# Attention scores on two opposite 64x64 quarters of the array, from the queries as loaded

## The chip, the cores and the metric

The kernel runs on one core of a Trainium2 chip (trn2). The metric is the device time of one execution in microseconds, the median of several runs. Its engines are named as in the profile: PE (TensorE; PEld are its weight loads), DVE (VectorE), ACT (ScalarE), POOL (GpSimd) and SP (SyncE, which here only starts transfers).

## What is computed

The reference chains an attention and two mixtures of experts. Only the attention is touched here:

```python
def _attn_ref(q, k, v):                      # 4 batches, 8 heads, 768 positions, 64 wide
    block, window = (32, 16)
    k_sum = k.reshape(B, H, nb, block, D).max(axis=3)
    v_sum = v.reshape(B, H, nb, block, D).mean(axis=3)
    scores_l = scale * q @ k^T               # only where |i - j| < window
    scores_s = scale * q @ k_sum^T + log(block)
    a = softmax(concat(scores_l, scores_s))
    return a @ concat(v, v_sum)
...
x = moe(attention)      # top-1 routing, 8 experts, tokens with a positive skip score
x = moe2(x)             # capacity-bound routing, 8 experts
```

So a query sees 31 neighbouring keys and the 24 block maxima of its head; its output is a mean over the neighbouring values and the 24 block means.

## The kernel before

`phase_a` computes the attention in eight units (a batch and one of two groups of four heads) of six steps each, 48 steps in all. Partitions 0 to 63 hold the 64 dimensions of one pair of heads, partitions 64 to 127 those of the other pair, so a tile row carries two heads at once. `load(u)` starts a unit's transfers on SP: keys `kt`, queries `qd`, values for the means `vt` (a `wraw` tile), and values for the product `VV`.

A step is a software pipeline; loop i emits on each engine, in this order, `qk(i)`, `ptr(i-2)`, `ex(i-1)`, `pv(i-3)`, then the work behind the attention:
- `qk` (lines 121 to 130): four score matmuls into `s_ps`. The 128 stationary columns are 64 queries of head A and 64 of head B; the moving operand has 118 columns, 24 block maxima and 94 neighbouring keys. VectorE adds the mask and takes the maximum (line 129).
- `ex` (131): ScalarE's exponentials. `ptr` (137): four transposes into `pt_ps`, ScalarE copies them to `pt_sb`. `pv` (144): eight product matmuls into `o_ps`, 64 columns wide, on the two column halves in turn; VectorE divides by the row sum into `X`.
- `post` (162) and `logits` (168): for odd units, whose tile then holds all 512 columns, transposes of a finished row block, four 32-column matmuls with the routing weights, and one more transpose. The bank `l_ps` exists once.

Since one stationary operand holds both heads, it has to be block diagonal: `Q2` holds zeros in two quarters (memset, line 69), and `prep_q` (106) copies the loaded queries into the other two, one half by ScalarE and one by VectorE. Keys are needed at offsets 64 columns apart, each with the 24 maxima in front, so `prep_k` (95, VectorE) takes the maxima, `prep_k2` (98) copies the neighbouring keys of odd windows into `K2`, and `prep_kc` (102, lines 104 and 105) copies the maxima in front of the windows in `kt` and `K2`. For units 2 to 7 all of these are VectorE's except one half of `prep_q`; the tables `SHIFT1` and `SHIFT` say in which step of the unit before they are emitted.

The block means: `add_v` (109) halves `vt` five times (VectorE for units 0 and 1, POOL after), `mean_v` (114) turns the sums with two transposes into an `l_ps` bank (line 117), ScalarE scales them (118), and three POOL copies spread them into `VV` (119). `AT_S` and `AT_M` say in which loop; both are emitted ahead of `pv`. In loop 5, `spin` keeps PE at work with four matmuls on the identity (line 243).

```python
229    AT_S={2:0,6:1,**{NT*u-5:u for u in range(2,8)}}; AT_M={3:0,7:1,**{NT*u-2:u for u in range(2,8)}}
...
244        if i in AT_S: add_v(AT_S[i])
245        if i in AT_M: mean_v(AT_M[i])
246        for j in pvs.get(i,[i-LB] if q+3<=i<n+LB else []): pv(j)
247        logits(i-PL-1)
```

After step 47 the routing, the gathered first expert layer (`phase_b`) and the second one (`phase_d`) follow; they start from the attention's last rows.

Of the kernel before, what the change touches and what calls it, by code (L numbers as in the profile page):

```python
# [11 lines left out]
NT=6  # L12
# [5 lines left out]
WARM=11; KEEP=(5,4)  # L18
SHIFT1=(2,3,3,3,4); SHIFT=(0,2,2,1,4)
# [30 lines left out]
def phase_a(nc,tc,ctx,I,st):  # L50
# [8 lines left out]
    Q2=[]; VV=[]; K2=[cp.tile([128,2,NT,118],F32,name=f"K2_{i}") for i in range(2)]  # L59
# [6 lines left out]
    for i in range(2):  # L66
        t=cp.tile([128,2,12,128],F32,name=f"Q2_{i}"); Q2.append(t)
        for h in range(2):
            (G if i else V).memset(t[0:64,h,:,64:128],0.0); G.memset(t[64:128,h,:,0:64],0.0)
# [8 lines left out]
    def load(u):  # L78
        b,g=units[u]
        kt=ld.tile([128,2,KW],F32,name="kt",bufs=3); qd=ld.tile([128,2,S],F32,name="qd"); vt=st["raw"].tile([128,2048],F32,name="wraw")  # L80
        vv=VV[u%3]; src=I['v65']
        def ld_k(h0,h1): nc.sync.dma_start(kt[:,h0:h1],I['k'][b,:,2*g+h0:2*g+h1,:])
        def ld_q(h0,h1): nc.sync.dma_start(qd[:,h0:h1],I['q'][b,:,2*g+h0:2*g+h1,:])
        def ld_v():
            nc.sync.dma_start(vt[:,0:1536],I['vt'][b,:,g])
        def ld_vv():
            for s0 in (0,2): nc.sync.dma_start(vv[24:24+VP,3*s0:3*s0+6].rearrange("p (a s) h d -> p a (s h d)",s=3),src[b,g,:,s0:s0+2,0:780])
        U[u]=dict(kt=kt,qd=qd,vt=vt,vv=vv,q2=Q2[u%2],k2=K2[u%2])
        U[u]['ks']=wk.tile([128,2,24],F32,name="ks",bufs=2)
# [16 lines left out]
    def prep_q(u,h,half,cpy):  # L106
        d=U[u]; qd,q2=d['qd'],d['q2']; r=64*half
        cpy(q2[r:r+64,h,:,r:r+64],qd[r:r+64,h].rearrange("p (t c)->p t c",c=64))  # L108
# [5 lines left out]
    def mean_v(u):  # L114
        d=U[u]; vt=d['vt']; ms=vt[0:24,1536:1792]
        p=ps.tile([128,4,128],F32,name="l_ps",bufs=1)
        for h in range(2): T.transpose(p[0:24,h,:],vt[:,1800+24*h:1824+24*h],ident)
        A.mul(ms.rearrange("p (h d)->p h d",d=128),p[0:24,0:2,:],1.0/32)  # L118
        for w in (0,4,8): G.tensor_copy(d['vv'][0:24,w:w+4,:,0:64],ms.rearrange("p (h d)->p h d",d=64)[:,None].to_broadcast([24,4,4,64]))  # L119
    X={}; XT={}; D={}  # L120
    def qk(i):
        u,pairs=steps[i]; d=U[u]
        p=ps.tile([128,4,128],F32,name="s_ps")
        for j,(h,w) in enumerate(pairs):
            T.matmul(p[:,j,0:118],d['q2'][:,h,w,:],d['k2'][:,h,w//2,:] if w%2 else d['kt'][:,h,64*w:64*w+118],start=True,stop=True)  # L125
# [42 lines left out]
    def logits(i):  # L168
# [3 lines left out]
        if not (now or old): return  # L172
# [49 lines left out]
    def first(u,h):  # L222
        prep_k(u,h); prep_k2(u,h,A.copy); prep_kc(u,h,V.tensor_copy)
        prep_q(u,h,0,A.copy); prep_q(u,h,1,V.tensor_copy)
# [4 lines left out]
    AT_S={2:0,6:1,**{NT*u-5:u for u in range(2,8)}}; AT_M={3:0,7:1,**{NT*u-2:u for u in range(2,8)}}  # L229
    splits={-1:((0,1),),0:((0,2),(0,3)),1:((1,0),(1,1)),2:((1,2),(1,3))}  # L230
    for i in range(n+PL+3):
# [11 lines left out]
        if i==KEEP[0]: spin(KEEP[1],ident.bitcast(BF)[:,None,:].to_broadcast([128,2,256]))  # L243
        if i in AT_S: add_v(AT_S[i])
        if i in AT_M: mean_v(AT_M[i])
        for j in pvs.get(i,[i-LB] if q+3<=i<n+LB else []): pv(j)
# [7 lines left out]
        if i<n and u and u+1<8:  # L254
# [881 lines left out]
```

## Time and profile before

| | |
|---|---|
| median of 3 runs | 668.12 us (667.36 to 669.19) |
| the profiled execution | 666.73 us |
| its span | 664.8 us |
| mean granted TensorE clock | 0.949 |
| PE busy | 597.6 us (90%) |
| VectorE busy | 457.9 us (69%) |
| ScalarE busy | 326.7 us (49%) |
| POOL busy | 363.3 us (55%) |
| weight loads (PEld) busy | 489.3 us (74%) |

The execution's own time is 1.9 us above its span, the first to the last instruction. Busy shares are averages over stages: the attention takes about the first quarter of the span, and there the waits between engines have to be read step by step. A matmul's end is modelled, and matmuls overlap, so the distance between starts tells what one costs, not its duration.

### The profile page before, as it was taken

Reading aid. Unit: us, or ns where it says so; the run is one execution under the profiler, and the core shown is the slowest. Engines: PE = TensorE matmul, PEld = TensorE weight load, DVE = VectorE, ACT = ScalarE, POOL = GpSimd, SP = SyncE. Lnnn points to the kernel's source line nnn. Section 1 sums busy time; section 2 is a strip of 40 time slices with the busy share of each in tenths; the row PEclk is TensorE's granted clock in tenths of the full one; section 3 lists DMA queues with packets and bytes.
Section 4 is the critical chain, followed back from the end, with each engine's and each line's share of the span. In section 5 each row is a group of like instructions: output and inputs, shape, how many; then the busy total and the mean of one; then the engine's idle time right before and its main releaser. Section 6 shows DMA issues by size and latency. Waiting matters only on the chain.

```text
span 664.8 us, 12679 instructions
## 1 busy us (share of the span) xinstructions
PE 597.6 (90%) x4465; PEld 489.3 (74%) x4468; DVE 457.9 (69%) x1689; ACT 326.7 (49%) x712; POOL 363.3 (55%) x395
## 2 busy tenths in 40 slices
PE   7859898998889999998349979999999999999994
PEld 4747776877567777775328869788887978898983
DVE  7957898889887799693876736677776767652110
ACT  5646685786644856661035144261625445363510
POOL 3163455162146388972038086393948759397941
PEclk9877898999989999999579999999999999999998
DMA  8997577505616978710071450907245170845000
GB/s 283 338 301 221 186 281 206 179 2 216 247 33 218 363 261 267 235 67 25 1 229 74 158 191 1 326 23 267 83 164 182 62 275 17 300 172 193 33 17 32
DMA packets 47616, 111.83 MB, mean 168 GB/s; under 512 B 3937, under 2 KB 4705, under 8 KB 47552
## 3 DMA queue, kind: packets, MB, share of 16 engines
q1 hardware_dynamic: 38992, 85.87, 38.4%
q0 software_dynamic: 6208, 20.39, 9.0%
q10 hardware_dynamic: 2352, 4.76, 2.0%
q8 instruction: 36, 0.59, 0.4%
q14 instruction: 28, 0.23, 0.1%
HBM read 96.53 MB, written 14.88 MB: 168 GB/s over the span
## 4 chain that ended last, share of the span: by engine, by line
PE 60%; DVE 14%; DMA 7%; issue 7%; ACT 6%; POOL 5%; POOLq 0%; SPq 0%; DVEq 0%; ACTq 0%
PE dh_ps L964 7%; PE dh_ps L965 6%; PE dh_ps L966 6%; PE dz_ps L981 5%; PE dz_ps L983 5%; PE dz_ps L982 5%; PE s_ps L125 4%; DMA qd<-in_q_dram 3%; POOL wl L935 2%; DMA wraw<-in_vt_dram 2%; ACT p_e L135 2%; PE h_ps L568 2%; PE o_ps L151 2%; DVE wl L506 2%; PE z_ps L591 2%
## 5 line engine op out<-in xcount | busy, mean ns | idle before, releaser
L935 POOL TENSOR_TENSOR wl<-wraw,wh 128x512 fp32r<-128x512 f32 x124 | 155.5, 1288 | 9.1 <-ACT wh L926 8.6
L964 PE MATMUL dh_ps<-dxh,wh 128*128 128x384 f32 x256 | 91.9, 359 | 2.1 <-ACT dxh L956 2.1
L965 PE MATMUL dh_ps<-dxl,wh 128*128 128x384 f32 x256 | 87.9, 343 | 0.6 <-DVE dxl L956 0.6
L966 PE MATMUL dh_ps<-dxh,wl 128*128 128x384 f32 x256 | 87.1, 340 | 0.0
L981 PE MATMUL dz_ps<-wh,dhh 128*128 128x512 f32 x192 | 78.8, 411 | 0.0
L983 PE MATMUL dz_ps<-wh,dhl 128*128 128x512 f32 x192 | 76.0, 396 | 0.0
L982 PE MATMUL dz_ps<-wl,dhh 128*128 128x512 f32 x192 | 76.0, 396 | 0.0
L926 ACT CAST wh<-wraw 128x512 fp32r<-128x512 f32 x128 | 73.5, 619 | 2.8 <-DMA wraw<-in_w1b_dram 2.8
L970 DVE SCALAR_TENSOR_TENSOR dhl<-dh_ps,dhh 128x384 fp32r<-128x384 f32 x64 | 35.5, 555 | 54.5 <-ACT dhh L969 54.4
L988 POOL DMA_INDIRECT out_dram<-dz,io x24 | 24.5, 1022 | 86.6 <-ACT dz L986 84.4
L969 ACT ACTIVATE dhh<-dh_ps 128x384 fp32r<-128x384 f32 x64 | 31.4, 491 | 78.8 <-PE dh_ps L966 67.8
L135 ACT ACTIVATE p_e<-s_sb,nm 128x118 f32<-128x118 f32 x192 | 59.7, 385 | 0.0
L119 POOL COPY VV<-wraw 24x1024 f32<-24x1024 f32 x24 | 24.3, 1044 | 60.9 <-ACT wraw L118 60.9
L986 ACT COPY dz<-dz_ps 128x512 f32<-128x512 f32 x24 | 14.1, 587 | 85.5 <-PE dz_ps L983 60.2
L506 POOL TENSOR_TENSOR wl<-wraw,wh 128x1024 fp32r<-128x1024 f32 (+1 forms) x18 | 37.6, 2115 | 27.6 <-ACT wh L505 27.6
L505 ACT CAST wh<-wraw 128x1024 fp32r<-128x1024 f32 (+1 forms) x56 | 48.9, 933 | 6.1 <-DMA wraw<-in_w1a_dram 4.3
L964 PEld LDWEIGHTS dh_ps<-dxh,wh 128*128 128x128 f32 x256 | 48.8, 191 | 2.7 <-ACT dxh L956 2.4
L965 PEld LDWEIGHTS dh_ps<-dxl,wh 128*128 128x128 f32 x256 | 48.8, 191 | 2.4 <-DVE dxl L956 2.3
L506 DVE TENSOR_TENSOR wl<-wraw,wh 128x1024 fp32r<-128x1024 f32 (+1 forms) x38 | 44.9, 1219 | 5.5 <-ACT wh L505 5.4
L966 PEld LDWEIGHTS dh_ps<-dxh,wl 128*128 128x128 f32 x256 | 48.6, 190 | 0.0
L125 PE MATMUL s_ps<-kt,Q 128*128 128x118 f32 x192 | 42.0, 302 | 6.5 <-ACT Q L108 2.1
L142 ACT COPY pt_sb<-pt_ps 118x512 f32<-118x512 f32 x48 | 28.0, 584 | 37.2 <-PE pt_ps L140 37.2
(350 smaller groups left out, 1435.9 us busy)
## 6 DMA issues: line engine op xcount, KB each, us to landing
wraw<-in_w1b_dram SPq DMA_DIRECT2D x16, 1024.0 KB, 5.1
wraw<-in_w2b_dram SPq DMA_DIRECT2D x14, 1024.0 KB, 9.3
wraw<-in_w2a_dram SPq DMA_DIRECT2D x12, 1024.0 KB, 7.9
wraw<-in_w1a_dram SPq DMA_DIRECT2D x10, 1024.0 KB, 5.8
VV<-in_v_dram SPq DMA_DIRECT2D x16, 585.0 KB, 9.9
kt<-in_k_dram SPq DMA_DIRECT2D x16, 412.0 KB, 7.0
qd<-in_q_dram SPq DMA_DIRECT2D x16, 384.0 KB, 6.9
wraw<-in_vt_dram SPq DMA_DIRECT2D x8, 768.0 KB, 8.9
```

The costliest lines, as they stand in the source:

```text
L125: T.matmul(p[:,j,0:118],d['q2'][:,h,w,:],d['k2'][:,h,w//2,:] if w%2 else d['kt'][:,h,64*w:64*w+118],start=True,stop=True)
L135: A.activation(pe[:,j,:],sb[:,j,:],AF.Exp,bias=nm[:,j:j+1],scale=-1.0)
L505: (hi.tensor_copy if hi else nc.scalar.copy)(h[:,c],t[:,c])
L506: (lo or nc.vector).tensor_tensor(l[:,c],t[:,c],h[:,c].bitcast(F32),op=OP.subtract)
L926: A.copy(h[:,c],t[:,c])
L935: eng.tensor_tensor(l[:,c],t[:,c],h[:,c].bitcast(F32),op=OP.subtract)
L964: T.matmul(q,wh[:,c],s['xh'][:,d,:],start=(d==0),stop=False)
L965: T.matmul(q,wh[:,c],s['xl'][:,d,:],start=False,stop=False)
L966: T.matmul(q,wl[:,c],s['xh'][:,d,:],start=False,stop=(d==3))
L981: T.matmul(q,s['hh'][:,f,c0],wh[:,c],start=(f==0),stop=False)
L982: T.matmul(q,s['hh'][:,f,c0],wl[:,c],start=False,stop=False)
L983: T.matmul(q,s['hl'][:,f,c0],wh[:,c],start=False,stop=(f==7))
```

## The change

`Q2` and `prep_q` go. The score matmul is split into two, one per head: contraction over 64 partitions and 64 stationary columns each, on the quarter of the array with rows 0 to 63 and columns 0 to 63 and on the one with rows 64 to 127 and columns 64 to 127. Both read the queries as loaded. `qd` gets a third buffer, since the scores now read it. All `prep_k2` and `prep_kc` are ScalarE's, for every unit, and one step each. `mean_v` is split: `turn_v` writes its two transposes into the second half of the bank that `logits` has open in that loop, and the scaling follows the copy of the logits. `add_v` moves one loop later (`AT_S`), and both it and the turning come behind `pv`. The four `spin` matmuls of loop 5 go.

```diff
--- before.py
+++ after.py
@@ -15,8 +15,8 @@
 VR=S+32; VP=96
 ROW=516
 NEG=-8e9
-WARM=11; KEEP=(5,4)
-SHIFT1=(2,3,3,3,4); SHIFT=(0,2,2,1,4)
+WARM=11
+SHIFT1=(2,3,4); SHIFT=(0,2,3)
 EARLYK={4:6,6:8}
 STAGES=(1,4,6,7,8); STAGES3=(2,2,3,3,4,5,5,7)
 LAGS=(1,2,3)
@@ -56,17 +56,13 @@
     cst=cp.tile([128,482],F32,name="cst")
     ident=cst[:,354:482]; mask=cst[:,:354].rearrange("p (m j)->p m j",m=3)
     w17=cp.tile([128,83],F32,name="w17")
-    Q2=[]; VV=[]; K2=[cp.tile([128,2,NT,118],F32,name=f"K2_{i}") for i in range(2)]
+    VV=[]; K2=[cp.tile([128,2,NT,118],F32,name=f"K2_{i}") for i in range(2)]
 
     wm=K2[1][:,0].rearrange("p a b->p (a b)")[:,0:256]; V.memset(wm,1.0); wm=wm.bitcast(BF)
     def spin(k,wm=wm):
         p=ps.tile([128,4,128],F32,name="s_ps").rearrange("p a b->p (a b)")
         for _ in range(k): T.matmul(p,wm[:,0:128] if len(wm.shape)==2 else wm[:,0,0:128],wm,start=True,stop=True)
     spin(WARM)
-    for i in range(2):
-        t=cp.tile([128,2,12,128],F32,name=f"Q2_{i}"); Q2.append(t)
-        for h in range(2):
-            (G if i else V).memset(t[0:64,h,:,64:128],0.0); G.memset(t[64:128,h,:,0:64],0.0)
     for i in range(3):
         t=cp.tile([24+VP,12,4,65],F32,name=f"VV_{i}")
         G.memset(t[0:24,:,:,64:65],1.0); VV.append(t)
@@ -77,7 +73,7 @@
     U={}
     def load(u):
         b,g=units[u]
-        kt=ld.tile([128,2,KW],F32,name="kt",bufs=3); qd=ld.tile([128,2,S],F32,name="qd"); vt=st["raw"].tile([128,2048],F32,name="wraw")
+        kt=ld.tile([128,2,KW],F32,name="kt",bufs=3); qd=ld.tile([128,2,S],F32,name="qd",bufs=3); vt=st["raw"].tile([128,2048],F32,name="wraw")
         vv=VV[u%3]; src=I['v65']
         def ld_k(h0,h1): nc.sync.dma_start(kt[:,h0:h1],I['k'][b,:,2*g+h0:2*g+h1,:])
         def ld_q(h0,h1): nc.sync.dma_start(qd[:,h0:h1],I['q'][b,:,2*g+h0:2*g+h1,:])
@@ -85,7 +81,7 @@
             nc.sync.dma_start(vt[:,0:1536],I['vt'][b,:,g])
         def ld_vv():
             for s0 in (0,2): nc.sync.dma_start(vv[24:24+VP,3*s0:3*s0+6].rearrange("p (a s) h d -> p a (s h d)",s=3),src[b,g,:,s0:s0+2,0:780])
-        U[u]=dict(kt=kt,qd=qd,vt=vt,vv=vv,q2=Q2[u%2],k2=K2[u%2])
+        U[u]=dict(kt=kt,qd=qd,vt=vt,vv=vv,k2=K2[u%2])
         U[u]['ks']=wk.tile([128,2,24],F32,name="ks",bufs=2)
         ld_k(0,1); ld_q(0,1)
         if u==0: nc.sync.dma_start(cst,I['cst'])
@@ -103,26 +99,24 @@
         d=U[u]; kt=d['kt']; ks=d['ks'][:,h,None,:].to_broadcast([128,NT,24])
         cpy(kt[:,h,0:768].rearrange("p (t j)->p t j",j=128)[:,:,0:24],ks)
         cpy(d['k2'][:,h,:,0:24],ks)
-    def prep_q(u,h,half,cpy):
-        d=U[u]; qd,q2=d['qd'],d['q2']; r=64*half
-        cpy(q2[r:r+64,h,:,r:r+64],qd[r:r+64,h].rearrange("p (t c)->p t c",c=64))
     def add_v(u):
         vt=U[u]['vt']; w=768
         while w>=48:
             e=V if u<2 else G
             e.tensor_tensor(vt[:,0:w] if w>48 else vt[:,1800:1848],vt[:,0:w],vt[:,w:2*w],op=OP.add); w//=2
-    def mean_v(u):
+    def turn_v(u,l):
+        for h in range(2): T.transpose(l[0:24,2+h,:],U[u]['vt'][:,1800+24*h:1824+24*h],ident)
+    def mean_v(u,l):
         d=U[u]; vt=d['vt']; ms=vt[0:24,1536:1792]
-        p=ps.tile([128,4,128],F32,name="l_ps",bufs=1)
-        for h in range(2): T.transpose(p[0:24,h,:],vt[:,1800+24*h:1824+24*h],ident)
-        A.mul(ms.rearrange("p (h d)->p h d",d=128),p[0:24,0:2,:],1.0/32)
+        A.mul(ms.rearrange("p (h d)->p h d",d=128),l[0:24,2:4,:],1.0/32)
         for w in (0,4,8): G.tensor_copy(d['vv'][0:24,w:w+4,:,0:64],ms.rearrange("p (h d)->p h d",d=64)[:,None].to_broadcast([24,4,4,64]))
     X={}; XT={}; D={}
     def qk(i):
         u,pairs=steps[i]; d=U[u]
         p=ps.tile([128,4,128],F32,name="s_ps")
         for j,(h,w) in enumerate(pairs):
-            T.matmul(p[:,j,0:118],d['q2'][:,h,w,:],d['k2'][:,h,w//2,:] if w%2 else d['kt'][:,h,64*w:64*w+118],start=True,stop=True)
+            for r in (0,64):
+                T.matmul(p[r:r+64,j,0:118],d['qd'][r:r+64,h,64*w:64*w+64],d['k2'][r:r+64,h,w//2,:] if w%2 else d['kt'][r:r+64,h,64*w:64*w+118],start=True,stop=True)
         sb=wk.tile([128,4,118],F32,name="s_sb"); nm=wk.tile([128,4],F32,name="nm")
         for j,(h,w) in enumerate(pairs):
             mk=mask[:,0 if w==0 else (2 if w==11 else 1),:]
@@ -169,12 +163,14 @@
 
 
         now,old=tile(i),tile(i-1)
-        if not (now or old): return
+        if not (now or old or i+PL+1 in AT_M): return
         l=ps.tile([128,4,128],F32,name="o_ps") if old==(B-1,NT-1) else ps.tile([128,4,128],F32,name="l_ps",bufs=1)
         if now:
             for k in range(4): T.matmul(l[32*k:32*k+32,0,:],w17[:,17*k:17*k+32],XT[now][:,k,:],start=True,stop=True)
         if old: T.transpose(l[:,1,:],XT.pop(old)[:,0,:],ident)
+        if i+PL+1 in AT_M: turn_v(AT_M[i+PL+1],l)
         if now: A.copy(XT[now][:,0,:],l[:,0,:])
+        if i+PL+1 in AT_M: mean_v(AT_M[i+PL+1],l)
         if old: V.tensor_reduce(st['lg'][:,old[0]*NT+old[1],:],l[:,1,:].rearrange("p (k j)->p j k",k=4)[:,0:17],AX.X,OP.add)
     def tile(j):
 
@@ -220,13 +216,12 @@
     zr=cp.tile([128,129],F32,name="zr"); G.memset(zr,0.0)
     load(0)
     def first(u,h):
-        prep_k(u,h); prep_k2(u,h,A.copy); prep_kc(u,h,V.tensor_copy)
-        prep_q(u,h,0,A.copy); prep_q(u,h,1,V.tensor_copy)
+        prep_k(u,h); prep_k2(u,h,A.copy); prep_kc(u,h,A.copy)
     first(0,0)
     n=len(steps)
     LE,LA,LB=LAGS; PL=LB+1
     q=LB+2; pvs={q:[0],q+1:[1,2],q+2:[3,4]}
-    AT_S={2:0,6:1,**{NT*u-5:u for u in range(2,8)}}; AT_M={3:0,7:1,**{NT*u-2:u for u in range(2,8)}}
+    AT_S={2:0,6:1,**{NT*u-4:u for u in range(2,8)}}; AT_M={3:0,7:1,**{NT*u-2:u for u in range(2,8)}}
     splits={-1:((0,1),),0:((0,2),(0,3)),1:((1,0),(1,1)),2:((1,2),(1,3))}
     for i in range(n+PL+3):
         u,t=(i//NT,i%NT)
@@ -240,10 +235,8 @@
             if i==0: first(0,1); load(1)
             if i==4: first(1,0)
             if i==5: first(1,1)
-        if i==KEEP[0]: spin(KEEP[1],ident.bitcast(BF)[:,None,:].to_broadcast([128,2,256]))
+        for j in pvs.get(i,[i-LB] if q+3<=i<n+LB else []): pv(j)
         if i in AT_S: add_v(AT_S[i])
-        if i in AT_M: mean_v(AT_M[i])
-        for j in pvs.get(i,[i-LB] if q+3<=i<n+LB else []): pv(j)
         logits(i-PL-1)
         if tile(i-PL): post(*tile(i-PL))
         for lag in range(10):
@@ -257,10 +250,8 @@
             if 0<=t-s[0]<2 and u not in (3,5): prep_k(u+1,t-s[0])
             for v,k in EARLYK.items():
                 if 0<=i-NT*v+k<2: prep_k(v,i-NT*v+k)
-            if 0<=t-s[1]<2: prep_k2(u+1,t-s[1],V.tensor_copy)
-            if 0<=t-s[2]<2: prep_q(u+1,t-s[2],1,V.tensor_copy)
-            if t in (s[3],s[3]+(2 if u>1 else 1)): prep_q(u+1,int(t>s[3]),0,A.copy)
-            if t==s[4]: prep_kc(u+1,0,V.tensor_copy); prep_kc(u+1,1,V.tensor_copy)
+            if 0<=t-s[1]<2: prep_k2(u+1,t-s[1],A.copy)
+            if 0<=t-s[2]<2: prep_kc(u+1,t-s[2],A.copy)
         if i<n and t==LB-1 and u+2<8:
             load(u+2)
         if i==7: nc.sync.dma_start(st['xrows'][0:128,:].rearrange("p (a c)->p a c",c=129),zr[:,None,:].to_broadcast([128,4,129])); st['load_const']()
```

How it moves instructions is seen at three places (in the changed kernel, lines stand 3 to 9 lower; `K` is `K2`, `Q` is `Q2`).

POOL, at loops 7 to 10, before. The additions are unit 2's (line 113), the copies spread the means of units 1 and 2 (`VV_126`, `VV_128`).
```order
L157 MEMSET X_340 128x6x4
L113 ISA
L113 TENSOR_TENSOR wraw<-wraw 128x768
L113 TENSOR_TENSOR wraw<-wraw 128x384
L113 TENSOR_TENSOR wraw<-wraw 128x192
L113 TENSOR_TENSOR wraw<-wraw 128x96
L113 TENSOR_TENSOR wraw<-wraw 128x48
L119 COPY VV_126<-wraw 24x16x64 x3
L119 COPY VV_128<-wraw 24x16x64 x3
```
The same place in the changed kernel, where unit 1's tile is `VV_116` and unit 2's is `VV_118`:
```order
L151 MEMSET X_341 128x6x4
L112 COPY VV_116<-wraw 24x16x64 x3
L106 ISA
L106 TENSOR_TENSOR wraw<-wraw 128x768
L106 TENSOR_TENSOR wraw<-wraw 128x384
L106 TENSOR_TENSOR wraw<-wraw 128x192
L106 TENSOR_TENSOR wraw<-wraw 128x96
L106 TENSOR_TENSOR wraw<-wraw 128x48
L112 COPY VV_118<-wraw 24x16x64 x3
```
Unit 1's copies now stand ahead of unit 2's additions.

VectorE, at loop 28, before: the division of a product, a reduction of the logits, the maxima of a later unit's keys, then the four copies of unit 5's maxima, and the next step's scores.
```order
L159 TENSOR_TENSOR X_1570<-o_ps,rc 128x256
L178 TENSOR_REDUCE lg<-l_ps 128x17
L97 TENSOR_REDUCE ks<-kt 128x24
L104 COPY kt<-ks 128x6x24
L105 COPY K_1_100<-ks 128x6x24
L104 COPY kt<-ks 128x6x24
L105 COPY K_1_100<-ks 128x6x24
L129 ISA s_sb,nm<-s_ps,cst 128x118
```
ScalarE, at loops 27 and 28, in the changed kernel: L97 is the key copy, L100 and L101 those of the maxima, L136 and L129 the copy and exponentials of the steps, L172 the copy of the logits, L111 the scaled means.
```order
L161 COPY xT<-xt_ps 128x512
L97 COPY K_1_100<-kt 128x6x94
L100 COPY kt<-ks 128x6x24
L101 COPY K_1_100<-ks 128x6x24
L136 COPY pt_sb<-pt_ps 118x512
L129 ACTIVATE p_e<-s_sb,nm 128x118 x4
L172 COPY xT<-l_ps 128x128
L111 ACTIVATE wraw<-l_ps 24x256
L100 COPY kt<-ks 128x6x24
L101 COPY K_1_100<-ks 128x6x24
L136 COPY pt_sb<-pt_ps 118x512
```
The copies of keys and maxima have left VectorE's queue and stand in ScalarE's, between two steps' work, spread over two loops.

## Rows read from the trace of the kernel before

**Rows 1.** Table by stretch, 40 to 168 us (us, then busy time of each engine, clock).
```profile
40.00:168.00 128.00, 115.55 (x1408) 97.11 (x1409) 111.72 (x575) 88.49 (x252) 54.82 (x84) 0.92 0.61 197
```

**Rows 2.** Timeline of PE, a long step (start, us, engine, line, operation, count, idle before).
```profile
94.30 0.38 PE L125 MATMUL s_ps<-kt,Q 128*128 128x118 f32 x2
...
95.18 0.60 PE L140 MATMUL pt_ps<-cst,p_e 128*118 128x128 f32 x4
95.71 0.69 PE L151 MATMUL o_ps<-VV,pt_sb 118*64 118x65 f32 x16
96.33 0.42 PE L175 MATMUL l_ps<-xT,w 128*32 128x128 f32 x8
...
97.29 0.38 PE L125 MATMUL s_ps<-kt,Q 128*128 128x118 f32 x2
```

**Rows 3.** Timeline of PE, a short step.
```profile
79.68 0.48 PE L125 MATMUL s_ps<-kt,Q 128*128 128x118 f32 x2
79.99 0.39 PE L125 MATMUL s_ps<-K,Q 128*128 128x118 f32 x2
...
81.82 0.48 PE L125 MATMUL s_ps<-kt,Q 128*128 128x118 f32 x2
```

**Rows 4.** Timeline of PE's weight loads in the long step.
```profile
95.71 0.55 PEld L151 LDWEIGHTS o_ps<-VV,pt_sb 118*64 118x64 f32 x16 [0.17 <-issue]
...
96.68 0.14 PEld L176 LDWEIGHTS l_ps<-cst,xT 128*128 128x128 f32 x1 [0.20 <-issue]
```

**Rows 5.** Timeline of POOL, 30 to 45 us.
```profile
34.69 4.37 POOL L113 TENSOR_TENSOR wraw<-wraw 128x768 f32<-128x768 f32 x5 [15.79 <-DMA wraw<-in_vt_dram]
```

**Rows 6.** Timeline of PE, 33.5 to 44.5 us.
```profile
40.08 1.13 PE L151 MATMUL o_ps<-VV,pt_sb 118*64 118x65 f32 x16 [6.86 <-POOL VV L119]
...
43.85 0.47 PE L117 MATMUL l_ps<-cst,wraw 128*24 128x128 f32 x2
```

**Rows 7.** Table by stretch, 39 to 42 and 115 to 118 us.
```profile
39.00:42.00 3.00, 1.92 (x20) 1.80 (x21) 0.67 (x3) 0.00 (x0) 2.99 (x4) 0.50 1.03 383
...
115.00:118.00 3.00, 3.00 (x22) 2.84 (x19) 2.93 (x18) 1.82 (x6) 0.00 (x0) 0.50 1.00 328
```

**Rows 8.** Timeline of PE, first score matmuls of steps 12, 14, 18, 30, 32.
```profile
48.63 0.48 PE L125 MATMUL s_ps<-kt,Q 128*128 128x118 f32 x2 [0.22 <-DVE kt L104]
...
59.86 0.38 PE L125 MATMUL s_ps<-kt,Q 128*128 128x118 f32 x2
...
72.12 0.38 PE L125 MATMUL s_ps<-kt,Q 128*128 128x118 f32 x2
...
109.97 0.48 PE L125 MATMUL s_ps<-kt,Q 128*128 128x118 f32 x2 [0.27 <-DVE kt L104]
...
119.28 0.48 PE L125 MATMUL s_ps<-kt,Q 128*128 128x118 f32 x2
```

**Rows 9.** Timeline of VectorE, 107.9 to 112 us.
```profile
109.84 1.85 DVE L105 COPY K<-ks 128x144 f32<-128x144 f32 x1
111.61 0.22 DVE L104 COPY kt<-ks 128x144 f32<-128x144 f32 x1
```

**Rows 10.** Timeline of POOL, 106 to 115 us.
```profile
109.80 4.38 POOL L113 TENSOR_TENSOR wraw<-wraw 128x768 f32<-128x768 f32 x5
```

**Rows 11.** Waits of PE up to 170 us (in total, times, longest, us).
```profile
PE l_ps L175 <- ACT wraw L118: 3.7, 3, 1.2
```

**Rows 12.** One line's instructions (min/median/max ns): query copies, key copies, 128x128 copies.
```profile
L108 ACT COPY Q<-qd x16: 817/832/843, 5.1 to 143.4; 64x768 f32<-64x768 f32 x16
...
L101 ACT COPY K<-kt x4: 647/656/663, 4.1 to 21.3; 128x564 f32<-128x564 f32 x4
...
L177 ACT COPY xT<-l_ps x24: 238/247/299, 48.8 to 178.8; 128x128 f32<-128x128 f32 x24
```

**Rows 13.** Timeline of ACT, two short steps.
```profile
80.80 0.82 ACT L108 COPY Q<-qd 64x768 f32<-64x768 f32 x1
...
83.66 0.58 ACT L142 COPY pt_sb<-pt_ps 118x512 f32<-118x512 f32 x1 [0.41 <-PE pt_ps L140]
```

## The prediction

> **What bounds the kernel now.** I read the table by stretch first, then PE's timeline step by step, then who PE waits for. In the stretch from 40 to 168 us, steps 10 to 47 of the attention, PE is busy for 115.6 of 128 us and VectorE for 111.7 [rows 1]; two engines that look nearly full say little, so the steps have to be opened. In a long step, one that also turns a finished row block, PE starts one piece of work after another: scores at 94.30, transposes at 95.18, products at 95.71, logits at 96.33, the next scores at 97.29, a period of 2.99 us [rows 2]. In a short step, without that work, the period is 2.14 us [rows 3]. PE waits for nobody there, so undisturbed steps are PE's. Not all steps are undisturbed, and there the others come in:
>
> - At 40.08 PE has waited 6.86 us for a product, for POOL's copies of the means [rows 6]. POOL itself stood for 15.79 us until the transfer of unit 2's `vt` had landed, added for 4.37 us up to 39.06, and only then copied the means of unit 1, which PE needed [rows 5]. The copies are simply behind the additions in POOL's order. In the 3 us after that, PE's granted clock is 0.50, the 1.2 GHz level [rows 7].
> - Around units 2, 3 and 5, VectorE's copies of the block maxima are late. One takes 1.85 us, the next of the same size 0.22 us [rows 9]; the slow one runs while POOL adds [rows 10]. PE's next scores wait for these copies at 48.63 and 109.97 [rows 8]. After the wait at 110 to 112 us the clock is 0.50 for another stretch, at full busy [rows 7]. Steps 12 and 13 take 11.23 us from 48.63 to 59.86, steps 18 and 19 take 7.56 from 72.12 to 79.68, steps 30 and 31 take 9.31 from 109.97 to 119.28 [rows 3, 8].
> - Three times the logits wait 1.2 us, 3.7 in total, for ScalarE's scaling of the means, which frees the one `l_ps` bank [rows 11].
>
> **What goes.** Part by part, against the profiled execution of 666.7 us:
>
> The start. Work before the 39.06 us at which POOL has added unit 2's values is bounded by a transfer, and none of its bytes change; so the memsets, the loop 5 `spin`, the query copies and whatever the scores cost up to there count nothing. If that cover were gone, the 6.86 us of idle would be the most they could be worth. POOL's copies for unit 1 now come ahead of the additions, so the product in loop 9 runs at once. What is late next is the turning of unit 2's sums in loop 10: PE stands there until 39.06 where it came to the same place at 43.85 [rows 6], 4.8 us earlier, and with the product of that loop, 0.62 [rows 2], already behind it: 5.4. PE still stands idle before that: 6.86 us, less the 1.0 from 39.06 to 40.08, less 2.7 for a product, scores, transposes and a product [rows 2] that no longer wait, some 3 us. So I take the slow clock again, for the 3 us of [rows 7] and a little more, 4 us at half speed, which costs 2: net **3.4**, up to 5.4 if the clock stays.
>
> The late copies. With key copies and maxima off VectorE, steps 12 and 13 should take two long periods, 5.98, steps 18 and 19 and steps 30 and 31 two short ones, 4.28 each: 5.25, 3.28 and 5.03, idle time and the slow clock after it. Unit 2's last copies are emitted only in loop 11, behind two copies of ScalarE's, so I leave half a microsecond of the first: **13.1** together.
>
> The bank. The turned sums lie in the logits' bank, and the logits come before them: **3.7**. VectorE's other work gets freer too; since PE bounds the undisturbed steps, that counts nothing there.
>
> Sum of the gains: 20.2 us.
>
> **What comes.** ScalarE. Units 2 to 7 bring it 12 key copies of 0.656 us and 24 copies of maxima; the nearest row for these is the 128x128 copy, 0.247 us, and by its length I take 0.26; 12 query copies of 0.832 go [rows 12]. That is 7.9 + 6.2 - 10.0 = 4.1 us on a stretch in which it works for 88.5 of 128 us [rows 1]. It stays below PE, so I cost it at nothing: the cover is ScalarE's idle time, 0.41 us in a short step [rows 13], and the slack of a step between its copy of the transposes and the products that read it. Were that cover gone, it would be 1.18 us per half unit, 12 times: 14.1.
>
> The scores on PE. Today a score matmul shows as two passes, and four of them take 0.88 us, 0.11 a pass of 118 columns [rows 2]. Now there are 16 passes. The nearest row is the product, whose two column halves take turns the same way: 16 passes of 65 columns in 0.62 us [rows 2], 0.039 each. By the columns' ratio 16 passes would take 1.13 us; less the change of shape counted below, 0.50 us x 118/65 = 0.91. So eight pairs at today's price of a pass: the time of the scores **stays**. The upper bound is passes one behind another, 1.76 us; that is a rival. Below, nothing excludes a few hundredths a step, at most 2 us in all.
>
> Changes of the array's shape. Between transposes and products PE's weight loads stand for 0.17 us with nothing to wait for, between logits and the last transpose for 0.20; between scores and transposes, which have the same shape today, they do not [rows 4]. The first score matmul after a product takes 0.31 us to the next one [rows 3] instead of 0.22, which is 0.09 more. So a change costs 0.09 to 0.20 us; I take 0.12, near the row that shows it before scores. A new one stands between scores and transposes in every step; where the step ends with 128-column transposes, another stands before the next scores. From step 12 to 46, 23 steps get two and 12 get one: 58 changes, **7.0** us (5.2 to 11.6). The Trainium skill has the rule that speaks against this change: changing the tiling mode drains the engine (TensorEngine Tiling (Array Packing), Key Properties). By that rule every one of the 58 costs; without it the sum would be 648, with it 655; the idle 0.17 and 0.20 us [rows 4] agree with it.
>
> Sum: 666.7 - 20.2 + 7.0 = 653.5 us. The median of the runs before stands 1.4 us above the profiled execution, so I predict **655 us** for the median. What follows the attention starts from its last rows and so moves with it. Bounds of the same case: 651 (clock stays at the start, 0.09 a change) to 663 (0.20 a change, and 3 us of other waits in the new order).
>
> **The rivals.**
>
> A: the two quarters do not run side by side. For it: no row shows two row halves at work together; the products share all their rows. Against it: those products do run side by side in one bank. The price is eight more passes of 0.11 us in each of 35 steps, 30.8 us: **686 us**, slower. It decides from the point where the scores take 0.38 us more than today, 1.26 us a step; there the gain of 13.2 is spent. A rule in the Trainium skill says this outright: different row tiles cannot access the same PSUM bank at once (TensorEngine Tiling (Array Packing), Gotcha 1), and both quarters write `s_ps` in one bank, if on different partitions. No trace here shows whether partitions save it. Chance 0.16.
>
> B: ScalarE becomes the bound. The step's ring of copy, exponentials and transposes has little slack in short steps [rows 13], and copies are now in it. If all of them lie open, 14.1 us: **669 us**, no change. Against it: query copies of 0.83 us stood in the same places; one lies at 80.80 [rows 13], in a step that lasted 2.14 us all the same [rows 3]. Chance 0.08.
>
> C: a change of shape costs nothing where it is already behind another wait, and the clock stays at the start: 655 - 7.0 - 2.0 = **646 us**. Against it: the idle of [rows 4] lies in full steps. Chance 0.06.
>
> **How the numbers follow.** My forecast has 0.70, A 0.16, B 0.08, C 0.06. A difference under 0.3%, 2 us, could not be told from none. Faster by more than that is the forecast and C, 0.76; within it is B, 0.08; slower is A, 0.16. The range goes from 645, below C, to 667, above the forecast's upper bound and into B: outside are A and half of B, two in ten.
>
> **What would show it.** Right: PE's scores of a step within 0.8 to 1.0 us, weight loads idle behind scores by 0.1 to 0.2; no wait of PE on VectorE's copies; a wait on POOL's additions near 39 us in loop 10; step 32's scores some 15 us before their 119.28 [rows 8] (20.2 less the last bank wait of 1.2, less 34 changes of shape, 4.1). Wrong: scores of 1.3 us and more (A); PE waiting for exponentials in steps with key copies (B); or a first experts' stage that starts no earlier, because its weights' transfer and not the attention would set it.

## The result and the profile after

The changed kernel takes **658.24 us** (median of 4 runs, 656.58 to 659.57) against 667.74 us for the kernel before beside it: a ratio of 0.9855, 95% interval 0.9825 to 0.9885. That is 9.5 us faster. The prediction was 655 us in a range of 645 to 667, faster; so the sign and the range hold, and 3 us are missing. The profiled execution took 659.57 us, its span is 657.6. Of all the runs below, one of `means_alone` (669.36 us, at a lower clock) counts as slow and is left out of its median and ratio.

Lines have moved in the changed kernel: scores are L119, transposes L134, products L145, logits L169, the turning of the sums L108, additions L106, scaling L111, copies of the means L112.

The table by stretch (us, then busy time of PE, PEld, VectorE, ScalarE and POOL, PE's clock, DMA share, GB/s), as [rows 1, 7]: from the first scores of step 10 to those of step 47, first in the kernel before, then in the changed one, and three stretches at the start of the changed one.

```profile
41.15:162.03 120.88, 109.12 (x1310) 92.01 (x1309) 106.57 (x543) 84.16 (x240) 51.98 (x78) 0.92 0.59 185
33.45:153.29 119.84, 107.22 (x1608) 82.76 (x1604) 87.52 (x504) 89.48 (x270) 54.16 (x82) 0.96 0.70 209
...
39.00:42.00 3.00, 0.00 (x0) 0.00 (x0) 0.00 (x0) 0.00 (x0) 2.79 (x3) 0.75 1.10 319
42.00:45.00 3.00, 2.17 (x14) 1.77 (x16) 0.00 (x0) 1.05 (x3) 1.77 (x4) 0.50 0.95 342
45.00:48.00 3.00, 3.00 (x40) 2.23 (x36) 0.99 (x9) 1.76 (x6) 3.00 (x8) 0.61 1.03 373
```

VectorE is busy 19.1 us less, ScalarE 5.3 us more (4.1 was forecast). The forecast took 0.26 us for a copy of the maxima on ScalarE; it takes 0.311 (min/median/max ns):

```profile
L100 ACT COPY kt<-ks x16: 292/311/323, 5.3 to 139.2; 128x144 f32<-128x144 f32 x16
```

PE still stands idle from 39 to 42 us; its clock falls meanwhile, and in the 3 us after that it is 0.50, the 1.2 GHz level.

The timeline of PE, a long step of the changed kernel (start, us, engine, line, operation, count), as [rows 2]:

```profile
88.16 0.42 PE L119 MATMUL s_ps<-kt,qd 64*64 64x118 f32 x4
88.42 0.37 PE L119 MATMUL s_ps<-K,qd 64*64 64x118 f32 x4
88.62 0.37 PE L119 MATMUL s_ps<-kt,qd 64*64 64x118 f32 x4
88.82 0.37 PE L119 MATMUL s_ps<-K,qd 64*64 64x118 f32 x4
89.12 0.65 PE L134 MATMUL pt_ps<-cst,p_e 128*118 128x128 f32 x4
89.70 0.69 PE L145 MATMUL o_ps<-VV,pt_sb 118*64 118x65 f32 x16
...
91.37 0.32 PE L119 MATMUL s_ps<-kt,qd 64*64 64x118 f32 x2
```

Sixteen passes take 0.96 us, from 88.16 to 89.12, where eight took 0.88 [rows 2]: the quarters work side by side. The long step has a period of 3.21 us instead of 2.99. Short steps mostly take 2.15 or 2.16, for 2.14 [rows 3]. PE's weight loads now stand idle before the scores and between scores and transposes, by 0.17 and 0.15 us (0.1 to 0.2 was forecast); the timeline of the weight loads, as [rows 4], in a short step and in this long one:

```profile
70.70 0.51 PEld L134 LDWEIGHTS pt_ps<-cst,p_e 128*118 128x118 f32 x4 [0.15 <-issue]
...
88.16 0.19 PEld L119 LDWEIGHTS s_ps<-kt,qd 64*64 64x64 f32 x4 [0.17 <-issue]
...
89.12 0.41 PEld L134 LDWEIGHTS pt_ps<-cst,p_e 128*118 128x118 f32 x4 [0.15 <-ACT xT L161]
```

Who PE waits for, up to 165 us (in total, times, longest):

```profile
PE l_ps L108 <- POOL wraw L106: 7.2, 1, 7.2
PE s_ps L119 <- ACT kt L100: 2.9, 3, 2.1
PE pt_ps L134 <- ACT p_e L129: 2.1, 3, 1.2
...
PE s_ps L119 <- DVE rs L147: 1.3, 3, 0.9
PE l_ps L340 <- ACT wraw L111: 1.2, 1, 1.2
```

The three waits for the logits' bank [rows 11] and the waits on VectorE's key copies [rows 8] are gone. The wait of 1.2 us for a scaling at L340, a matmul of the routing, is not new: before, that matmul (L349) waited 1.2 us in two pieces. The wait at the start is not gone: it stands on POOL's addition, and is 7.16 us where it was 6.86 [rows 6]. The timelines of POOL and then of PE at that place, as [rows 5, 6], with the first scores of step 12:

```profile
38.41 4.37 POOL L106 TENSOR_TENSOR wraw<-wraw 128x768 f32<-128x768 f32 x5 [5.64 <-DMA wraw<-in_vt_dram]
```
```profile
34.99 0.69 PE L145 MATMUL o_ps<-VV,pt_sb 118*64 118x65 f32 x16
42.83 0.60 PE L108 MATMUL l_ps<-cst,wraw 128*24 128x128 f32 x2 [7.16 <-POOL wraw L106]
...
48.72 0.42 PE L119 MATMUL s_ps<-kt,qd 64*64 64x118 f32 x4
```

The addition, which waits for its transfer, began at 38.41 instead of 34.69.

By the first score matmul of each step, the changed kernel is ahead by 7.7 us at step 10, by nothing at step 12 (48.72 against 48.63), by 3.5 at step 13, 7.3 at 19, 10.1 at 31, 8.4 at 33 and 8.7 at step 47. What follows step 47 takes 504.3 us here and 502.8 before.

### The profile page after: what moved, and what is told of

It reads as the page before. It is cut to its first block, busy times and chain, and to the rows that moved or that the text cites. A ratio compares the mean times of both kernels' runs of the same rounds, so it can differ in the third digit from the quotient of the medians.

```text
span 657.6 us, 13424 instructions
## 1 busy us (share of the span) xinstructions
PE 601.8 (92%) x4845; PEld 480.7 (73%) x4848; DVE 432.8 (66%) x1627; ACT 329.0 (50%) x740; POOL 356.7 (54%) x389
## 4 chain that ended last, share of the span: by engine, by line
PE 38%; issue 5%; POOL 3%; DVE 3%; DMA 1%; ACT 1%; POOLq 0%; DVEq 0%; ACTq 0%
PE dh_ps L955 7%; PE dh_ps L956 6%; PE dh_ps L957 6%; PE dz_ps L972 5%; PE dz_ps L974 5%; PE dz_ps L973 5%; POOL wl L926 2%; DMA xg<-xrows,p_ix 1%; PE dh_ps L944 1%; PE rt_ps L802 1%; POOL out_dram L979 1%; DVE p_g L793 1%; PE rt_ps L800 1%; ACT dxh L947 0%; ACT wh L917 0%
## 5 line engine op out<-in xcount | busy, mean ns | idle before, releaser
L112 POOL COPY VV<-wraw 24x1024 f32<-24x1024 f32 x24 | 23.9, 1030 | 70.2 <-ACT wraw L111 70.2
L129 ACT ACTIVATE p_e<-s_sb,nm 128x118 f32<-128x118 f32 x192 | 59.8, 386 | 0.3 <-DVE nm L123 0.3
L123 DVE CUSTOM_DVE_ANT_0 s_sb<-s_ps,cst 128x118 f32<-128x118 f32 x192 | 42.1, 275 | 18.8 <-PE s_ps L119 17.8
L933 POOL DMA_INDIRECT xg<-xrows,p_ix x24 | 23.3, 972 | 38.2 <-DVE rrow L867 23.9
## 6 DMA issues: line engine op xcount, KB each, us to landing
VV<-in_v_dram SPq DMA_DIRECT2D x16, 585.0 KB, 13.2
```

The source lines that it names most:

```text
L123: V.tensor_tensor_reduce(out=sb[:,j,:],in0=p[:,j,0:118],in1=mk,scale=-0.125,scalar=3e38,op0=OP.add,op1=OP.min,accum_out=nm[:,j:j+1])
L129: A.activation(pe[:,j,:],sb[:,j,:],AF.Exp,bias=nm[:,j:j+1],scale=-1.0)
```

## The experiments

Times are medians, ratios stand against runs of the kernel before on the same chip in the same session, brackets are 95% intervals. "Step 47" is the start of its scores in one profiled execution; before it is 162.03, in the change 153.29. What follows took 500.7 to 510.9 us in single traces, with stretches at the low clock after 300 us in different places (from 300 to 360 us the mean is 0.72 in the change and 0.81 in `late_turn2`), so a median's last microseconds are not the attention's.

The theory had three parts: what was missing was lost at the start, to the late load and the wait in loop 10; the quarters bring nothing by themselves; and VectorE's late work beside POOL has only changed its name. Against each stands a rival in the expectations below.

### Each part alone, in the kernel before

**Scores on the quarters only** (`scores_alone`)

```diff
-T.matmul(p[:,j,0:118],d['q2'][:,h,w,:],...)
+for r in (0,64):
+    T.matmul(p[r:r+64,j,0:118],d['qd'][r:r+64,h,64*w:64*w+64],...)
-prep_q(u+1,...)   (all of them, and the Q2 tiles; qd gets 3 buffers)
```

> The kernel before with the quarter scores alone: Q is used as loaded, so its copies are gone; the key copies stay on VectorE and the turning in its own bank. Theory (the quarters cost about 0.22 us in each long step and 0.1 in each short one, some 5 us in all, and pay only by the VectorE copies of Q that go away): between 664 and 671 us, the wait on VectorE's copy of the even keys before step 32 shorter than before but still there. Rival (the quarters and the missing copies are what made the change faster): 660 or below.

669.43 us, ratio 0.9993 [0.9958, 1.0028]: nothing, as the theory had it. The wait for VectorE's key copies did not get shorter, though: 1.8 us in step 30, for 1.9 before. And the trace has a loss and a gain: step 12 begins 4.1 us later than before, steps 12 and 13 then take 7.56 us instead of 11.23.

**Key copies by ScalarE only** (`keys_alone`)

```diff
-prep_k2(u+1,t-s[1],V.tensor_copy); prep_kc(u+1,...,V.tensor_copy)
+prep_k2(u+1,t-s[1],A.copy); prep_kc(u+1,t-s[2],A.copy)   (tables as in the change)
-prep_q(u+1,...,0,A.copy)
+prep_q(u+1,...,0,V.tensor_copy)
```

> The kernel before with all key copies by ScalarE, as in the change, and both halves of Q by VectorE; scores on the whole array, turning in its own bank. Theory (the gain of the change is that late key copies no longer stand behind VectorE's work beside the additions): 655 to 661 us, no wait of TensorE on a VectorE copy before steps 12, 18 and 32. Rival (what remains on VectorE is as late, so only all three parts together give it): 664 or above.

659.79 us, 0.9837 [0.978, 0.9895], in the theory's range. Steps 18 and 30 take 2.03 us instead of 4.89 and 5.48, step 12 takes 4.29 instead of 7.48. No step waits for a key copy of VectorE's any more: the late copies were what they seemed.

**The turning in the logits' bank only** (`means_alone`)

```diff
-p=ps.tile([128,4,128],F32,name="l_ps",bufs=1)
-for h in range(2): T.transpose(p[0:24,h,:],vt[...],ident)
+for h in range(2): T.transpose(l[0:24,2+h,:],vt[...],ident)
 (after the logits; products ahead of the additions; additions at 6u-4)
```

> The kernel before with the turning of the means in the logits' bank alone. Theory: the waits of the logits on ScalarE's scaling, 3.7 us in the trace of before, go, and at the start nothing is gained because TensorE waits for the addition of unit 2 wherever the turning stands: 662 to 667 us. Rival (the start gains the 3.4 us of the prediction too): 658 to 661.

659.99 us (five runs), 0.9864 [0.9799, 0.9929]: the rival's range. Here the start does gain: step 12 begins at 44.58, 4.05 us earlier than before. The timeline of PE there, in this kernel, and the first scores of step 12:

```profile
39.44 0.39 PE L115 MATMUL l_ps<-cst,wraw 128*24 128x128 f32 x2 [2.46 <-POOL wraw L113]
...
44.58 0.38 PE L125 MATMUL s_ps<-kt,Q 128*128 128x118 f32 x2
```

POOL's addition began at 34.64, as before, and PE was released when it ended. That is the prediction's start (39.06 was forecast), in a kernel without quarter scores.

The product of the three ratios is 0.9696; the change has 0.9855. So 1.6%, over 10 us, is lost where the parts meet. (All three keep the four `spin` matmuls of loop 5, which the change drops; no run moves these alone.)

The traces say where. By step 47 the three parts gain 18.7 us together and the change 8.7, so 10.0 are missing; of these only 0.7 by step 12. Most, 7.6, is steps 12 and 13: each part alone shortens them, by 3.7, 4.0 and 4.2 us, and the change by 4.2, once. Steps 30 to 32 make 5.1 (parts 1.2, 4.3 and 1.2, change 1.6), and the other steps give 3.4 back. The parts largely remove the same waits, so their gains do not add.

### What the quarters cost

**The change with whole-array scores again** (`scores_undone`): block-diagonal Q, both halves copied by VectorE.

```diff
-T.matmul(p[r:r+64,j,0:118],d['qd'][r:r+64,...],...)   (for r in (0,64))
+T.matmul(p[:,j,0:118],d['q2'][:,h,w,:],...)
+prep_q(u+1,t-s[1],0,V.tensor_copy); prep_q(u+1,t-s[1],1,V.tensor_copy)   (with the Q2 tiles; qd has 2 buffers)
```

> The changed kernel with the scores of before (block-diagonal queries, four 128x128 matmuls), both query copies by VectorE; key copies and means as changed. Theory (the quarters cost PE 0.21 us in each long step by two more changes of shape and nothing in short ones): long steps go back to 2.99 us, about 4.5 us of gain in all, unless the 24 pairs of query copies, 1.1 us a pair and more beside POOL, make scores late: 654 to 659 us. Rival (the quarters themselves bring the gain): 664 us or more, with long steps no shorter than 3.2 us.

658.25 us, 0.9834 [0.9791, 0.9877]: as the change itself, and in the theory's range. Long steps take 2.99 us again, steps 16, 28 and 40 take 2.77 instead of 2.99, steps 18, 30 and 42 take 2.03 instead of 2.16. Its step 47 came at 150.20, so its trace gained 3.1 us that the median does not show.

**One quarter after the other** (`quarters_apart`)

```diff
-for j,(h,w) in enumerate(pairs):
-    for r in (0,64):
+for r in (0,64):
+    for j,(h,w) in enumerate(pairs):
```

> The change with the two quarters' score matmuls one quarter after the other (all eight pairs on the upper quarter, then all on the lower) instead of alternating. Theory (the alternating order is what lets the two quarters work at once): a set of 16 takes about 1.7 us instead of 0.95, long steps 3.9 to 4.0 us, 685 to 700 us. Rival (the engine overlaps them anyway): 0.95 to 1.1 us a set, 655 to 661 us.

677.42 us (two runs), 1.0132 [1.0046, 1.0218], slower than before. PE's timeline in one set:

```profile
68.30 0.41 PE L119 MATMUL s_ps<-kt,qd 64*64 64x118 f32 x2
68.55 0.36 PE L119 MATMUL s_ps<-K,qd 64*64 64x118 f32 x2
68.75 0.42 PE L119 MATMUL s_ps<-kt,qd 64*64 64x118 f32 x4
68.95 0.42 PE L119 MATMUL s_ps<-K,qd 64*64 64x118 f32 x4
69.21 0.36 PE L119 MATMUL s_ps<-kt,qd 64*64 64x118 f32 x2
69.41 0.36 PE L119 MATMUL s_ps<-K,qd 64*64 64x118 f32 x2
69.71 0.65 PE L134 MATMUL pt_ps<-cst,p_e 128*118 128x128 f32 x4
```

1.41 us a set: the first 0.45 us has one quarter alone (counts of 2), then both (4), then the other alone. The second quarter's first pass started when four of the first quarter's eight had begun, no earlier. So neither forecast is right: the two overlap, but only over a part of the set. Long steps take 3.66 us and short ones 2.61, some 0.45 more each. Steps 12 to 14 lose another 7.6 us, at the low clock. The timeline of PE before them, and this kernel's table by stretch,

```profile
41.39 0.60 PE L108 MATMUL l_ps<-cst,wraw 128*24 128x128 f32 x2 [3.78 <-POOL wraw L106]
```
```profile
44.00:56.00 12.00, 12.00 (x93) 8.79 (x89) 3.70 (x24) 5.44 (x18) 7.83 (x21) 0.50 1.03 281
56.00:68.00 12.00, 12.00 (x98) 9.61 (x98) 4.90 (x25) 4.84 (x13) 0.00 (x0) 0.54 0.54 166
```

show PE idle for 3.78 us, then full and at 0.50, the 1.2 GHz level, for most of 24 us, where the change is at 1.00 again from 48 us on.

### The start

**Turning unit 2 three loops later** (`late_turn2`)

```diff
-AT_M={3:0,7:1,**{NT*u-2:u for u in range(2,8)}}
+AT_M={3:0,7:1,13:2,**{NT*u-2:u for u in range(3,8)}}
```

> The changed kernel with the sums of unit 2 turned in loop 13 instead of loop 10. Theory (PE's 7.2 us of idle in loop 10 is only the place in PE's order; nothing PE needs before loop 13 is missing): the idle goes and with it the slow clock behind it, 7 to 9 us, about 650 us. Rival (the transfers bound this stage anyway): PE, or VectorE ahead of it, waits for the keys of unit 3 in loops 12 and 13 or for the products of unit 2 in loop 15 instead, and the time is 655 to 658 us.

650.34 us, 0.975 [0.9703, 0.9798], as the theory had it. The addition began as late as in the change, but PE does not stand for it. POOL's timeline, the first scores of step 12 and the table by stretch of this run:

```profile
38.16 4.40 POOL L106 TENSOR_TENSOR wraw<-wraw 128x768 f32<-128x768 f32 x5 [4.78 <-DMA wraw<-in_vt_dram]
```
```profile
39.99 0.42 PE L119 MATMUL s_ps<-kt,qd 64*64 64x118 f32 x4
```
```profile
36.00:39.00 3.00, 3.00 (x54) 2.41 (x49) 2.93 (x19) 3.00 (x10) 0.84 (x1) 1.00 1.03 198
39.00:42.00 3.00, 2.08 (x33) 1.36 (x28) 0.85 (x5) 2.69 (x10) 2.77 (x4) 1.00 1.08 297
42.00:45.00 3.00, 3.00 (x50) 2.30 (x48) 1.97 (x13) 2.22 (x7) 1.83 (x8) 1.00 1.03 348
```

The clock stays at 1.00 and step 12 begins at 39.99, 8.7 us earlier than in the change; at step 47 it is 10.4. This is more than the start was worth in any part alone: it takes away PE's wait for unit 2's addition, which the kernel before and `means_alone` have as well (6.86 and 2.46 us).

**Two buffers for the loaded Q** (`qd2`). In the ten traces taken before this run, the five kernels with quarter scores had moved 10.8 to 11.3 MB by 38 us, the five others 11.5 to 11.6. The change gave Q a third buffer.

```diff
-qd=ld.tile([128,2,S],F32,name="qd",bufs=3)
+qd=ld.tile([128,2,S],F32,name="qd")
```

> The change with two buffers for the loaded Q, as before, instead of three; everything else as in the change. Theory (the third buffer, or where it lets the tiles lie, is why all five kernels with quarter scores have moved 10.8 to 11.3 MB by 38 us and the five without 11.5 to 11.6): the addition of unit 2 starts at 34.3 to 36.3 instead of 38.4, TensorE's wait in loop 10 falls from 7.2 to 3 to 5, 654 to 657 us. Rival (the scores themselves or the earlier start of unit 0 slow the loads): the addition at 37 or later, 657 to 661 us.

659.33 us, 0.9852 [0.9786, 0.9918], the addition at 39.48. The rival's ranges, and the theory falls.

**The Q tiles of before kept, unread** (`q2_kept`, on top of `qd2`)

```diff
+t=cp.tile([128,2,12,128],F32,name=f"Q2_{i}"); Q2.append(t)
+(G if i else V).memset(t[0:64,h,:,64:128],0.0); G.memset(t[64:128,h,:,0:64],0.0)
```

> The change with two buffers for the loaded Q (as in the run of that name) and with the two block-diagonal Q tiles of before allocated and cleared again, though nothing reads them; scores on the quarters. Theory (that these 24 KB per partition are gone, and the other tiles lie elsewhere, slows the first loads): the addition of unit 2 starts at 34.3 to 36.3, 11.4 MB or more moved by 38 us. Rival (the scores on the quarters, or the earlier start of unit 0 with no Q copies, do): the addition at 37 or later, 10.8 to 11.2 MB.

658.72 us (two runs), 0.9811 [0.9783, 0.9839], the addition at 38.06, 11.0 MB by 38 us. Again the rival's ranges. The line of POOL's timeline in each run, first `qd2`, then `q2_kept`:

```profile
39.48 4.37 POOL L106 TENSOR_TENSOR wraw<-wraw 128x768 f32<-128x768 f32 x5 [6.65 <-DMA wraw<-in_vt_dram]
```
```profile
38.06 4.37 POOL L110 TENSOR_TENSOR wraw<-wraw 128x768 f32<-128x768 f32 x5 [5.19 <-DMA wraw<-in_vt_dram]
```

By these two traces neither the third buffer nor the place of the tiles delays that load. They are single traces, and the place of the landing varies: in the change and `early_adds`, which are alike up to loop 14, the addition begins at 38.41 and 36.32. Over all traces it begins at 36.3 to 40.0 us in the nine kernels with quarter scores and at 34.3 to 36.3 in the five without. What delays the load stays open: the scores themselves, or that unit 0 starts about 1 us earlier without its query copies (5.6 to 6.1 us against 6.8 to 7.1).

### VectorE beside POOL

In the change, VectorE's gate operations of units 3 and 5 are late. The timelines of VectorE, POOL and ScalarE at the second place (the last VectorE line is from a later unit):

```profile
104.44 0.20 DVE L184 TENSOR_REDUCE g_m<-lg 128x6 f32<-128x48 f32 x1
104.67 1.83 DVE L185 TENSOR_TENSOR g_d<-lg,g_m 128x48 f32<-128x48 f32 x1
...
106.55 0.99 DVE L332 TENSOR_SCALAR r_do<-lg 128x6 f32<-128x6 f32 x1
...
107.57 0.94 DVE L93 TENSOR_REDUCE ks<-kt 128x24 f32<-128x768 f32 x1
...
144.14 0.21 DVE L185 TENSOR_TENSOR g_d<-lg,g_m 128x48 f32<-128x48 f32 x1
```
```profile
104.64 1.80 POOL L106 TENSOR_TENSOR wraw<-wraw 128x768 f32<-128x768 f32 x1
...
106.51 0.99 POOL L106 TENSOR_TENSOR wraw<-wraw 128x384 f32<-128x384 f32 x1
```
```profile
106.53 0.24 ACT L186 ACTIVATE g_d<-g_d 128x48 f32<-128x48 f32 x1 [2.39 <-DVE g_d L185]
```

The subtraction `g_d` (0.21 us at 144.1, where POOL is idle) starts 0.03 us after POOL's addition of 1.80 and ends as that ends; `r_do` (0.16) does the same with the next addition, 0.99 to 0.99. ScalarE then stands 2.39 us for `g_d` with its exponentials behind it, and PE, with nothing to transpose, 1.23. Steps 31 and 32 take 4.38 and 3.30 us, where the prediction had two short ones. The reduction `ks`, 0.94 us at 107.57 beside further additions and 0.94 alone, is not held up. That is the rule in the Trainium skill, SBUF — State Buffer, Who interferes with whom: VectorE with two inputs in SBUF, or in a two-port mode, and GpSimd lock a common port pair for a whole instruction, and a reduction does not. The trace agrees for the subtraction, which has two inputs, and for the reduction; for `r_do` it shows the wait, but not in which mode the instruction ran.

**Additions of units 4 and 6 earlier** (`early_adds`)

```diff
-AT_S={2:0,6:1,**{NT*u-4:u for u in range(2,8)}}
+AT_S={2:0,6:1,8:2,14:3,15:4,26:5,27:6,38:7}
```

> The changed kernel with the additions for the means of units 4 and 6 emitted one loop after those of units 3 and 5 (loops 15 and 27 instead of 20 and 32), so that POOL does them before the copies of units 3 and 5 and is quiet when VectorE computes the gate. Theory (VectorE's small gate operations, up to 1.85 us each, are held up by POOL's additions and copies, and PE by them): steps 19 to 21 and 31 to 32 lose their excess of 1.0, 0.5, 2.2 and 1.1 us, so 658.2 becomes about 653.5 us. Rival (those operations are late for another reason, or PE would wait for something else there): 657 to 660 us. If unit 4's values land too late for it, PE waits in loop 21 and up to 2 us come back.

656.04 us, 0.9822 [0.9776, 0.9869], a little better than the rival's range and short of the theory's 653.5. In its trace steps 31 and 32 take 2.35 and 2.15 us instead of 4.38 and 3.30, steps 19 to 21 6.59 instead of 7.98: these waits do come from where POOL's additions fall. Step 47 comes at 147.49, 5.8 us earlier than in the change; of that, 1.8 is from the start, which the edit does not touch and where the addition began at 36.32. In the median only 2 us show, inside the interval.

**Both moves** (`both`): the two edits together.

> The two edits together. Theory: they lie in different loops and add, about 645.5 us. Rival: the earlier pace meets the transfers of units 4 and 5 (POOL's additions of unit 4 wait for them, with the copies of unit 3 behind), and less than the sum remains, 648 to 653 us.

651.83 us, 0.9771 [0.9725, 0.9817]: the rival's range, and no better than the late turning alone. POOL's timeline, then PE's:

```profile
64.54 4.41 POOL L106 TENSOR_TENSOR wraw<-wraw 128x768 f32<-128x768 f32 x5 [9.07 <-DMA wraw<-in_vt_dram]
68.88 2.99 POOL L112 COPY VV<-wraw 24x1024 f32<-24x1024 f32 x3
```
```profile
69.96 1.14 PE L145 MATMUL o_ps<-VV,pt_sb 118*64 118x65 f32 x16 [3.62 <-POOL VV L112]
```

With PE ahead, unit 4's addition stands 9.07 us for its load, unit 3's copies stand behind it in POOL's order, and the product behind them: the very pattern of [rows 5, 6], two units on.

**Late turning, and only unit 6's addition earlier** (`late2_add6`)

```diff
-AT_S={2:0,6:1,**{NT*u-4:u for u in range(2,8)}}
+AT_S={2:0,6:1,8:2,14:3,20:4,26:5,27:6,38:7}
 (and AT_M as in late_turn2)
```

> The change with the turning of unit 2 three loops later and the addition of unit 6 five loops earlier, so that GpSimd has it behind it before the V copies of unit 5. Theory (step 31 is late because VectorE's gate operations run beside GpSimd's copies and then its addition): steps 31 to 32 fall from 4.11 us to 2.2 to 3.5 and the total from 650.3 to 648.4 to 649.8. Rival (the addition waits for its load in front of the V copies, as in the run with both): 650 to 652 us.

649.30 us, 0.9717 [0.9665, 0.9769]. Step 31 takes 3.27 us instead of 4.11, but step 22 lost 1.25 (5.86 for 4.61), and step 47 is where it was (142.82 and 142.87). Not to be told from the late turning alone.

**Late turning with whole-array scores** (`late2_undone`): the edits of `late_turn2` and `scores_undone`.

> The change with the turning of unit 2 three loops later (as in the run that moved it alone) and with the scores back on the whole array and VectorE copying both halves of Q. Theory (quarters cost 0.22 us in each long step and up to 0.13 in each short one): step 47's scores 4 to 5 us earlier than with the late turning alone (142.87), 645 to 647 us. Rival (quarters and block-diagonal Q are worth the same, as the medians of the change and of the change without quarters say): 649 to 652, step 47's scores within 1.5 us of 142.87.

650.93 us, 0.9716 [0.9652, 0.978], step 47 at 142.83: the rival holds. The long steps do take 2.99 us here, 0.22 less than with quarters. But VectorE has Q to copy again, which shows in steps 11 (4.25 us for 3.10), 16 (3.71 for 2.99) and 32 (3.70 for 2.15). It comes to the same.

## Why the prediction held, and where it failed

The sum was 20.2 us of gains against 7.0 of costs, 13.2 net; by the trace the attention gained 8.7, and the medians 9.5.

- **The start, 3.4 us: failed.** "None of its bytes change" is true, but that the transfer would therefore land at the same time was the step that failed: in the change's trace the addition began 3.7 us later (1.6 later in `early_adds`, so the size varies), it ended at 42.78 and not at 39.06, and at step 12 nothing was left (48.72 against 48.63). Where the load came earlier the term was right: 4.05 us with the addition at 34.64 (`means_alone`), 2.97 with it at 35.69 (`scores_undone`). The step also hid a choice. It took for granted that PE must stand in loop 10 for the turning; `late_turn2` shows that this wait was worth 8.7 us at step 12.
- **The late copies, 13.1: partly.** Steps 12 and 13 fell from 11.23 to 7.06 us: 4.2 gained, 4.3 forecast (4.75 less four changes of shape). Steps 18 and 19 gained 2.2 of some 3.0, steps 30 and 31 gained 2.8 of some 4.8, and step 32 gave 1.2 back. Missing here is that the gate's small VectorE operations stand at the same places and under the same additions as the copies that were taken away. [Rows 9, 10] showed the pattern; the prediction read it as a matter of those copies. `early_adds` shows that these waits come from the additions.
- **The bank, 3.7: right.** Steps 16, 28 and 40 fell by 1.09 us each, and by 1.31 without quarters, 3.9 in all.
- **ScalarE, nothing: right in kind.** Its busy time grew by 5.3 us, 1.2 more than forecast, by the longer copies of the maxima. PE waited for its key copies 2.9 us in all: 0.36 and 2.10 at 18.7 and 21.4, under the cover of the start, and 0.42 at 49.8. The later short steps paid nothing; B is out.
- **The scores, unchanged: right.** 0.96 us, of which the first pass's change of shape is a part. A is out, though both quarters write one bank. The Trainium skill says that different row tiles cannot (TensorEngine Tiling (Array Packing), Gotcha 1); here pairs in one bank start 6 to 7 ns apart, and 16 passes take hardly longer than eight took. The measurement decides, for quarters that write different partitions. A's mechanism exists, in an order that the change did not choose: `quarters_apart`, 677 us.
- **58 changes of shape, 7.0: somewhat too much.** A long step has two and takes 0.22 us more, as forecast (0.24). Short steps pay 0.13 where they were at 2.03, and 0.01 to 0.04 where something else already held them at 2.11 to 2.14. Over the 25 steps that are undisturbed in both the change and `scores_undone`, with 45 changes between them, I add up 4.4 us, where 0.12 each makes 5.4. The other changes lie in steps that wait for something else, where their cost does not show.

The total looks better than its terms, and that is in part luck. By the trace of the attention, 7 to 8 us of gains did not come, and some 3 us went the other way: costs of the changes of shape that did not show (up to 2.6) and small gains elsewhere. After step 47 the traced execution lost another 1.5 us, which the medians do not show. The forecast for step 32, some 15 us earlier, shows the miss more plainly: it came 9.6 earlier.

## To carry to other kernels

When an engine stands for another's transfer, ask first whether it has to stand there at all: moving the waiting instruction behind work that is ready (the turning of unit 2, three loops) gave some 8 us, nearly as much as the whole change, without making anything faster. When copies that are slow under another engine's work are moved away, list what else the first engine does there, since it inherits the collision. And cost a part by its own run: the quarter scores gave nothing alone (0.9993) and nothing in the best versions, so the gain of the whole must not be put down to them. Do not add up such gains either: three parts each shortened steps 12 and 13 by about 4 us, and so did all three together.

## What was not expected of the hardware

- How far quarter matmuls overlapped went by their order: alternating, 16 passes take 0.96 us; eight passes of one and then eight of the other 1.41, with the second quarter starting 0.45 us in.
- With PE full from 44 to 68 us, its granted clock stayed near 0.50 in `quarters_apart` for most of that time; before, it had stood 3.8 us idle. In `late_turn2`, where it did not stand, the clock was 1.00 through the same stretch of the program.
- In the first 38 us, the nine kernels with quarter scores moved 10.8 to 11.3 MB and the five without them 11.5 to 11.6, with the same loads in the same order. By one trace each, neither Q's buffers nor the Q tiles explain it; the cause was not found.
